# Attention and two expert layers on one core: zeroing spread over four engines, scale products on ScalarE, and a planner that keeps VectorE and GpSimd apart

## The chip, the core and the metric

The kernel runs on one core of a Trainium2 chip. The metric is device microseconds from the first to the last instruction of one execution. Five engines work side by side and meet at semaphores: TensorE (PE for matmuls, PEld for the loads of their weights), VectorE (DVE), ScalarE (ACT), GpSimd (POOL) and SyncE (SP), which here only issues DMA transfers. Every engine takes its instructions in the order in which they stand in the program; one that waits holds up all behind it on that engine.

## What is computed

```
# 1. delta-rule attention, batch 4, 8 heads, 768 tokens, head_dim 48
k_n = k / (norm(k) + 1e-6)
for t in range(768):
    y[t]  = q[t] @ state
    v_old = k_n[t] @ state
    state = state + beta[t] * outer(k_n[t], v[t] - v_old)
# 2. first expert layer: 3072 tokens x 384, 8 experts of 1024, weights P
P = exp(x @ w_gate - max);  8 rounds of row and column normalisation
out = sum_e P[:, e] * (relu(x @ w1[e]) @ w2[e])
# 3. second expert layer: each token goes to its best expert only
```

## The kernel before

The attention runs over 24 blocks of 64 tokens (12 chunks of two pairs of batches). A block's work falls into a front part (norms of K, power-of-two scales for Q and V, splitting into two fp16 parts), the inverse of a 64x64 triangle by five levels of matmuls, and a part that carries the state. The nodes have names that the code gives them: `ssr` is the sum of squares of K, `rc1` to `rc5` the reciprocal of the norm, `kn` the scaled keys, `kh` and `kl` their two parts, `qh` and `ql` those of Q, `kpd` and `kb` the copies of keys into block-diagonal buffers, `z`, `Z`, `a`, `t`, `tt` one level of the inverse, `ds` and `S` the state, `mx` the largest output of a block, `is`, `si` and `lgs` the scale of the logits and the logits.

The block-diagonal buffers must hold zeros outside their blocks. There are four rotating sets (`zK`, `zQ`, `zT`, `zM`, `zP`, `zU`); the first set is zeroed by GpSimd, the others by DMAs from a tensor of zeros (L1297 to L1303).

While the attention runs, units of the first expert layer for tokens that are already done are woven into TensorE's order (L1089 and L1115), so that TensorE has work where the attention waits. Expert 0 needs its weights loaded, measured by sums of squares (L1188), scaled and split (L1226, L1228).

The order on every engine is made by a list scheduler in the program itself, `Sched`. Each node has a cost in nanoseconds, an engine or a choice of two, a priority and dependencies. `plan` always takes the node that can start first on its engine and writes the order down; the program then issues it so. On the chip nothing of the plan's times is left, only the order on each engine. Of 40 plans with shuffled priorities the one that does best in `late`, a second model with random delays, is taken. One node is a stand-in for a set-up of GpSimd that the plan prices at 9400 ns, `("lib", 0)`, with the operation of L1295.

After the attention come the eight normalisation rounds of P (about 34 us on VectorE, beside expert units on TensorE), the rest of the first layer in blocks (L534, L584), and the second layer.

Of the kernel before, what the change touches and what calls it, by code (L numbers as in the profile page):

```python
# [15 lines left out]
ALU = mybir.AluOpType  # L16
# [32 lines left out]
class Sched:  # L49
# [6 lines left out]
    SHUFFLE = 0.2  # L56

    def __init__(self, slots):
        self.free = {e: 0.0 for e in "PVAGD"}
        self.slots = {k_: [0.0] * n for k_, n in slots.items()}  # L60
        self.nodes = []
        self.names = {}
        self.warm = False
        self.tick, self.colsum = 0, 0.0
        self.credit, self.tlast = 0.0, 0.0
        self.log = []

    def node(self, eng, cost, fn, deps, prio=0.0, ps=None, cols=0, frees=None, moe=False, name="", floor=0.0, lat=0.0):
# [18 lines left out]
    def start(self, n, e):  # L87
        s = max(n.ready, self.free[e])
        if n.ps:
            fr = [x for x in self.slots[n.ps[0]] if x is not None]  # L90
            if not fr:
                return None
            s = max(s, min(fr))
        return s

    def run(self, draws=1):
# [4 lines left out]
        for k in range(draws):  # L101
# [3 lines left out]
            self.free, self.slots = dict(free), {k_: list(v) for k_, v in slots.items()}  # L105
            self.warm, self.tick, self.colsum, self.credit, self.tlast, self.log = False, 0, 0.0, 0.0, 0.0, []
# [43 lines left out]
    def plan(self):  # L150
# [3 lines left out]
        while left:  # L154
# [55 lines left out]
            self.free[e] = end  # L210
            self.log.append((n.name, e, s, end))
# [19 lines left out]
def kernel(  # L231
# [412 lines left out]
    def mk_pe(e, key=None, iv=None):  # L644
        iv = e if iv is None else iv
        a = pet[:, iv]
        nc.vector.tensor_tensor(out=a, in0=P[:, :, e], in1=isx, op=ALU.mult)
        nc.vector.tensor_scalar(out=a, in0=a, scalar1=ivt[:, iv:iv + 1], scalar2=None, op0=ALU.mult)
        pe[key or e] = a
# [10 lines left out]
    ND = 3  # L660
    ZF = {"zK": 0.0, "zQ": 0.0, "zT": 1800.0, "zM": 3600.0, "zP": 4200.0, "zU": 5000.0}
# [3 lines left out]
    with (  # L665
# [20 lines left out]
        sch = Sched({"pz": 3, "pc": 2, "pt": 2, "py": 1})  # L686
# [53 lines left out]
        def block(i):  # L740
# [89 lines left out]
            N("par", "A", 200, lambda: nc.scalar.activation(out=o["sr"][:, 8:10], in_=o["sv"], func=AF.Sqrt), ["sv", "sq"], frees="sv")  # L830
            N("rc1", "V", 120, lambda: nc.vector.reciprocal(out=tl("rc", [8], F32, par), in_=o["sr"][:, 0:8]), ["sq", ("kn", i - 2)])
            N("rc2", "V", 80, lambda: nc.vector.tensor_tensor(out=o["rc"], in0=o["rc"], in1=o["ss"][:, 0:8], op=ALU.mult), ["rc1"])
            N("rc3", "V", 80, lambda: nc.vector.tensor_tensor(out=o["rc"], in0=o["sr"][:, 0:8], in1=o["rc"], op=ALU.add), ["rc2"])
            N("rc4", "V", 70, lambda: nc.vector.tensor_scalar(
                out=o["rc"], in0=o["rc"], scalar1=256.0 / 64, scalar2=1e-6 / 64, op0=ALU.mult, op1=ALU.add), ["rc3"])
            N("rc5", "V", 120, lambda: nc.vector.reciprocal(out=o["rc"], in_=o["rc"]), ["rc4"])
# [15 lines left out]
            else:  # L852
# [176 lines left out]
            N("is", "V", 70, lambda: nc.vector.tensor_tensor(out=isx[:, i:i + 1], in0=o["mx"][:, 0:1], in1=o["scl"][:, 7:8], op=ALU.mult), ["mp", "p4"], prio=tp)  # L1029
            N("si", "V", 70, lambda: nc.vector.tensor_tensor(out=o["scl"][:, 4:5], in0=isx[:, i:i + 1], in1=ivg, op=ALU.mult), ["is", ("lgs", i - 2)], prio=tp)  # L1030
# [21 lines left out]
            N("lgs", "V", 133, lambda: nc.vector.tensor_scalar(out=lg[:, i], in0=o["pl"], scalar1=o["scl"][:, 4:5], scalar2=None, op0=ALU.mult),  # L1052
# [1070 lines left out]
```

## Time and profile before

| what | us |
|---|---|
| median of 3 runs | 2105.6 (2104.56 to 2108.5) |
| profiled execution | 2101.38 |
| its span | 2099.2 |
| PE busy in the span | 1985.6 (95%) |
| DVE busy | 1387.7 (66%) |
| ACT busy | 1150.6 (55%) |
| POOL busy | 602.3 (29%) |

The attention's last logits are written at 604 us. "Busy" is the union of an engine's instructions. A PE that shows busy is not necessarily at its peak, since short matmuls overlap. In a line of a timeline the bracket at the end is the time for which the engine stood idle before the instruction, and what ended the wait.

### The profile page before, as it was taken

The numbers are of one execution on the slowest core, as the hardware profiler recorded it, in microseconds if no ns is written. First come the engines' busy times: TensorE is split into PE (matmuls) and PEld (weight loads), VectorE is DVE, ScalarE is ACT, GpSimd is POOL, SyncE is SP. The second block draws the span as 40 slices with busy tenths as digits, with TensorE's granted clock in tenths as the row PEclk, the third lists the DMA queues.
The fourth block names the chain that finished last, engine by engine and source line by source line (L and its number), as shares of the span: only waits on it lengthen the run. The fifth ranks groups of instructions, "written<-read, shape, count | busy, mean of one in ns | idle before, by whom it ended". The sixth has DMA issues, their size and how long they took to land. (4 is left out here: it accounts for less than half of the span.)

```text
span 2099.2 us, 55384 instructions
## 1 busy us (share of the span) xinstructions
PE 1985.6 (95%) x23391; PEld 1630.9 (78%) x23391; DVE 1387.7 (66%) x3045; ACT 1150.6 (55%) x2374; POOL 602.3 (29%) x524
## 2 busy tenths in 40 slices
PE   3779999999999999999999999999999999999998
PEld 3667777777775479999899989988999755567777
DVE  6988988988772776776767677676766555551111
ACT  6766665666532656666666656665665333433322
POOL 2232233223100123533533343353333201022211
PEclk9889999999999999999999999999999999999999
DMA  8355655546535113022032112302220010168765
GB/s 281 82 104 107 126 114 110 123 103 132 116 100 208 45 61 121 32 92 91 31 121 96 58 54 99 121 32 91 95 88 31 1 28 20 31 222 332 251 222 208
DMA packets 325982, 230.02 MB, mean 110 GB/s; under 512 B 258572, under 2 KB 303536, under 8 KB 319330
## 3 DMA queue, kind: packets, MB, share of 16 engines
q1 hardware_dynamic: 321442, 216.18, 34.7%
q0 software_dynamic: 4288, 10.25, 1.4%
q8 instruction: 185, 3.03, 0.6%
q14 instruction: 67, 0.55, 0.1%
HBM read 146.94 MB, written 50.36 MB: 94 GB/s over the span
## 5 line engine op out<-in xcount | busy, mean ns | idle before, releaser
L534 PE MATMUL pt<-big,W 128*128 128x256 f16 x4320 | 511.0, 273 | 0.0
L534 PEld LDWEIGHTS <-W 128*128 128x128 f16 x4320 | 418.5, 98 | 43.9 <-issue 0.3
L542 ACT ACTIVATE R<-pt 128x512 f32<-128x512 f32 x240 | 142.6, 594 | 306.9 <-PE pt L534 283.4
L525 POOL TENSOR_TENSOR R<-R,R 128x512 f32<-128x512 f32 x120 | 155.3, 1294 | 371.6 <-ACT R L542 288.2
L566 DVE SCALAR_TENSOR_TENSOR accb<-py,pet,accb 128x192 f32<-128x192 f32 x240 | 123.0, 513 | 203.8 <-PE py L584 203.3
L525 POOL TENSOR_TENSOR R<-R 128x512 f32<-128x512 f32 x120 | 161.6, 1346 | 195.3 <-ACT R L542 190.6
L584 PEld LDWEIGHTS <-A 128*128 128x128 f16 x2520 | 211.1, 98 | 7.2 <-DVE A L522 2.6
L1089 PE MATMUL pt<-accb,W 128*128 128x256 f16 (+1 forms) x1368 | 180.9, 272 | 3.5 <-ACT accb L729 1.8
L1115 PE MATMUL py<-W,hhl 128*128 128x384 f16 x756 | 152.6, 328 | 2.6 <-ACT yo L1125 1.7
L584 PE MATMUL py<-W,A 128*128 128x192 f16 x1440 | 134.7, 246 | 2.1 <-DVE accb L566 1.4
L1089 PEld LDWEIGHTS <-W 128*128 128x128 f16 x1368 | 118.3, 100 | 18.7 <-issue 3.8
L1635 PEld LDWEIGHTS <-W 128*128 128x128 f16 x1008 | 90.6, 98 | 51.1 <-issue 0.7
L584 PEld LDWEIGHTS <-hhl 128*128 128x128 f16 x1440 | 120.6, 98 | 5.9 <-DVE hhl L522 3.6
L1655 PE MATMUL py<-W,hhl 128*128 128x384 f16 x624 | 108.8, 326 | 0.0
L1641 DVE SCALAR_TENSOR_TENSOR ttb<-pt,ttb 128x512 f16<-128x512 f32 x50 | 34.6, 692 | 111.5 <-ACT ttb L1640 111.1
L584 PE MATMUL py<-W,hhl 128*128 128x192 f16 x1080 | 105.1, 246 | 2.8 <-DVE hhl L522 2.7
L1115 PEld LDWEIGHTS <-hhl 128*128 128x128 f16 x864 | 74.2, 98 | 40.8 <-DVE hhl L1102 3.2
L394 ACT ACTIVATE jk<-st 128x512 f32<-128x512 f32 x162 | 98.0, 605 | 13.7 <-DMA st<-in_moe_w_dram 11.4
L584 PE MATMUL py<-ew,A 128*128 128x192 f16 x1080 | 104.3, 246 | 0.6 <-DVE A L522 0.5
L522 DVE TENSOR_TENSOR A<-R,A 128x512 f16<-128x512 f32 x120 | 100.7, 841 | 2.9 <-ACT A L519 2.9
L584 PEld LDWEIGHTS <-ttb 128*128 128x128 f16 x1080 | 91.0, 98 | 9.9 <-issue 5.4
L1635 PE MATMUL pt<-big,W 128*128 128x512 f16 x432 | 97.7, 379 | 0.0
(411 smaller groups left out, 4090.4 us busy)
## 6 DMA issues: line engine op xcount, KB each, us to landing
st<-in_moe_w_dram SPq DMA_DIRECT2D x27, 1536.0 KB, 9.9
W<-w2d SPq DMA_DIRECT2D x18, 1536.0 KB, 8.2
w2d<-big SPq DMA_DIRECT2D x16, 1536.0 KB
big<-w2d SPq DMA_DIRECT2D x8, 1536.0 KB, 7.4
accb<-w2d SPq DMA_DIRECT2D x8, 1536.0 KB, 8.1
big<-accb SPq DMA_DIRECT2D x90, 128.0 KB, 3.6
accb<-in_kq_dram SPq DMA_DIRECT2D x23, 448.0 KB, 4.6
st<-PTc SPq DMA_DIRECT2D x42, 128.0 KB, 3.2
```

The costliest lines, as they stand in the source:

```text
L394: nc.scalar.activation(out=jk, in_=st[:, c * CW:c * CW + CW], func=AF.Square, scale=2.0 ** 0.5, accum_out=ss[:, c:c + 1])
L522: return lambda: nc.vector.tensor_tensor(out=A[2 * k + 1], in0=src, in1=A[2 * k], op=ALU.subtract)
L525: nc.gpsimd.tensor_tensor(out=out, in0=a, in1=b, op=op)
L534: nc.tensor.matmul(out=po, lhsT=w1v(W, wv, kk, f), rhs=xv[:, kk].rearrange("p (h n) -> p h n", h=2), start=kk == 0 and x == 0 and f % 2 == ...
L542: nc.scalar.activation(out=(R1, R)[y][:, :, o:o + 256], in_=pv if y else pv_, func=AF.Relu)
L566: nc.vector.scalar_tensor_tensor(out=acc[t][:, sl], in0=src, scalar=sc, in1=acc[t][:, sl], op0=ALU.mult, op1=ALU.add)
L584: nc.tensor.matmul(out=py, lhsT=A[2 * ka + a_][:, 128 * q_:128 * q_ + 128], rhs=B[2 * kb + b_][:, DH * q_:DH * q_ + DH], start=first and q ...
L1089: nc.tensor.matmul(out=o[g4][:, nt_ * j:nt_ * j + nt_], lhsT=w1v(W, wv, kk, f_), rhs=XR[:, xv, kk], start=(kk == 0 and x == 0), stop=(kk = ...
L1115: nc.tensor.matmul(out=o["py", j][:, 0:DM], lhsT=a_[f_ // per][:, c_:c_ + 128], rhs=w2v(W, b_, f_), start=(f_ == 0 and x == 0), stop=(f_ = ...
L1635: nc.tensor.matmul(out=po, lhsT=w1v(W, wv, kk, f), rhs=xv[:, kk, :], start=(kk == 0 and x == 0), stop=(kk == KD - 1 and x == 2))
L1641: V((f"rs{q_}", id_), lambda q_=q_: nc.vector.scalar_tensor_tensor(out=HL[q_], in0=o[q_], scalar=0.0, in1=HH[q_], op0=ALU.max, op1=ALU.sub ...
L1655: nc.tensor.matmul(out=o["py"][:, 0:DM], lhsT=a_[f // per][:, c_:c_ + 128], rhs=w2v(W, b_, f), start=(f == 0 and x == 0), stop=(f == KF - ...
```

## The change

Four things change in the attention's part.

1. Of the buffers that DMAs zeroed, four are zeroed by VectorE (`ZV`: set 1 of zK, zT, zQ, zM) and two by ScalarE (`ZA`: set 1 of zP and set 2 of zK). Ten DMAs of zeros stay of sixteen.
2. Four products of scales per block (`p3`, `p4`, `is`, `si`) go from VectorE to ScalarE. Two instructions of VectorE per block are folded away (`ssc` into a bias of the square root and other powers of two, `rc4` into `rc3`).
3. The matmul that adds squares over partitions (`sv`) takes bf16 operands instead of f32, and waits for ScalarE's sum alone and no more for VectorE.
4. `Sched` gets the flag `shared`. With it, an instruction of VectorE or GpSimd whose name is not in `ALONE` may not start in the plan before the other engine's last such instruction has ended.

```diff
+    ALONE = [x + y for x, n in (("Z", 6), ("m", 2), ("pt", 2), ("t", 6), ("rs", 4)) for y in "012345"[:n]] + [
+        f"tt{x}" for x in range(1, 6)] + ["r1", "r2", "U", "S", "mx", "lgs", "ssr"]
...
+        n.port = self.shared and name.split(".")[0] not in self.ALONE
...
         s = max(n.ready, self.free[e])
+        if n.port and e in "VG":
+            s = max(s, self.held["VG"[e == "V"]])
...
             self.free[e] = end
+            if n.port and e in "VG":
+                self.held[e] = end
...
+    onesb = res.tile([128, 128], BF16, name="onesb")
...
+    nc.gpsimd.memset(onesb, 1.0)
+    tiny = res.tile([128, 1], F32, name="tiny")
+    nc.gpsimd.memset(tiny, 1e-30)
...
+    ZV = (("zK", 1), ("zT", 1), ("zQ", 1), ("zM", 1))
+    ZA = (("zP", 1), ("zK", 2))
...
-        sch = Sched({"pz": 3, "pc": 2, "pt": 2, "py": 1})
+        sch = Sched({"pz": 3, "pc": 2, "pt": 2, "py": 1}, True)
...
-            N("ssc", "V", 70, lambda: nc.vector.tensor_scalar(
-                out=o["ss"], in0=o["ss"], scalar1=2.0 ** -18, scalar2=1e-30, op0=ALU.mult, op1=ALU.max), ["ssr", "sqv"])
-            N("sq", "A", 220, lambda: nc.scalar.activation(out=tl("sr", [10], F32, par)[:, 0:8], in_=o["ss"][:, 0:8], func=AF.Sqrt),
-              ["ssc", ("pq", i - 2), ("rc3", i - 2)])
+            N("sq", "A", 220, lambda: nc.scalar.activation(out=tl("sr", [10], F32, par)[:, 0:8], in_=o["ss"][:, 0:8], func=AF.Sqrt, bias=tiny),
+              ["ssr", ("pq", i - 2), ("rc3", i - 2)])
...
-                nc.tensor.matmul(out=o["sv"], lhsT=ones32, rhs=o["ss"][:, 8:10], start=True, stop=True)
-            N("sv", "P", 250, f, ["ssc"], ps=("pc", 1))
+                nc.tensor.matmul(out=o["sv"], lhsT=onesb, rhs=o["ss"].bitcast(BF16)[:, 17:20:2], start=True, stop=True)
+            N("sv", "P", 100, f, ["sqv"], ps=("pc", 1))
...
-            N("p3", "V", 75, lambda: nc.vector.tensor_tensor(
-                out=o["scl"][:, 5:6], in0=o["scl"][:, 1:2], in1=c3[:, 1:2], op=ALU.mult), ["pm", ("cs", 0)])
-            N("p4", "V", 70, lambda: stt(o["scl"][:, 7:8], o["scl"][:, 0:1], 0.125, o["scl"][:, 1:2], ALU.mult), ["pm"])
+            N("p3", "A", 170, lambda: nc.scalar.activation(out=o["scl"][:, 5:6], in_=o["scl"][:, 1:2], func=AF.Copy, scale=1.0 / 128), ["pm"])
+            N("p4", "A", 170, lambda: nc.scalar.activation(out=o["scl"][:, 7:8], in_=o["scl"][:, 0:1], func=AF.Copy, scale=o["scl"][:, 5:6]), ["p3"])
...
-            N("is", "V", 70, lambda: nc.vector.tensor_tensor(out=isx[:, i:i + 1], in0=o["mx"][:, 0:1], in1=o["scl"][:, 7:8], op=ALU.mult), ["mp", "p4"], prio=tp)
-            N("si", "V", 70, lambda: nc.vector.tensor_tensor(out=o["scl"][:, 4:5], in0=isx[:, i:i + 1], in1=ivg, op=ALU.mult), ["is", ("lgs", i - 2)], prio=tp)
+            N("is", "A", 170, lambda: nc.scalar.activation(out=isx[:, i:i + 1], in_=o["mx"][:, 0:1], func=AF.Copy, scale=o["scl"][:, 7:8]), ["mp", "p4"], prio=tp)
+            N("si", "A", 170, lambda: nc.scalar.activation(out=o["scl"][:, 4:5], in_=isx[:, i:i + 1], func=AF.Copy, scale=ivg), ["is", ("lgs", i - 2), ("wg3", 0)], prio=tp)
...
+                elif (nm, i) in ZV:
+                    Q((nm, i), "V", 150 + 0.45 * c_, lambda t=bufs[i]: nc.vector.memset(t.bitcast(F32), 0.0), [], -9.0)
+                elif (nm, i) in ZA:
+                    Q((nm, i), "A", 950, lambda t=bufs[i], c_=c_: nc.scalar.activation(
+                        out=t.rearrange("p a h k -> p (a h k)").bitcast(F32), in_=ones32[:, 0:1].to_broadcast([128, c_ // 2]), func=AF.Copy, scale=0.0), [], -9.0, floor=1300.0)
```

The plan comes out in another order on every engine. Three places at the start are shown. First ScalarE, from its first work on block 0 on. `accb` holds block 0's keys and queries and, in other columns, the loaded weights of expert 0, whose sums of squares go to `wmx`; `scl` holds the scales, `pz` is PSUM. Before:

```order
L813 ACTIVATE accb,ss<-accb 128x512
L806 ACTIVATE accb<-accb 128x384
L816 ACTIVATE accb,ss<-V 128x384
L822 ACTIVATE sr<-ss 128x8
L830 ACTIVATE sr<-sv 128x2
L729 CAST accb<-accb 128x384
L856 ACTIVATE V<-V,scl 128x384
L860 ACTIVATE accb<-accb,scl 128x8x64
L729 COPY big<-accb 64x16x48
L729 CAST accb<-pz 128x8x64 x2
```

And now:

```order
L844 ACTIVATE sr<-sv,tiny 128x2
L822 ACTIVATE accb<-hhl 128x384
L1200 ACTIVATE W_96,wmx<-accb 128x1024 x2
L869 ACTIVATE V<-V,scl 128x384
L873 ACTIVATE accb<-accb,scl 128x8x64
L745 CAST Rh<-V 128x384
L875 ACTIVATE scl<-scl 128x1
L1200 ACTIVATE W_96,wmx<-accb 128x1024
L876 ACTIVATE scl<-scl 128x1
L745 COPY big<-accb 64x16x48
L1200 ACTIVATE W_96,wmx<-W_97 128x768
L1212 ACTIVATE wma<-sw 128x1
```

Four squares of expert 0's weights (L1200), all of which wait for loads, now stand among the steps of block 0; the two zero fills stand ahead of this stretch, before block 0's first square, and the casts of block 0's keys out of PSUM (`pz`) one square behind it.

Second SyncE, from the ninth DMA on: `hhl<-in_kq_dram` loads block 1, `in_moe_w_dram` expert 0's weights, `in_zer_dram` are zeros. Before:

```order
L1276 DMA btok<-in_beta_dram 128x192
L1301 DMA st<-in_zer_dram 128x2048
L1301 DMA big<-in_zer_dram 128x2048
L1301 DMA ttb<-in_zer_dram 128x1024
L1175 DMA accb<-in_moe_w_dram 128x1024
L717 DMA big<-accb 64x16x64 x2
L800 DMA accb<-in_kq_dram 128x896
```

And now:

```order
L1288 DMA btok<-in_beta_dram 128x192
L816 DMA hhl<-in_kq_dram 128x896
L817 DMA V<-in_v_dram 128x384
L1187 DMA accb<-in_moe_w_dram 128x1024 x3
L1318 DMA ttb<-in_zer_dram 128x1024
L1289 DMA wg_s<-in_moe_w_gate_dram 128x3x8
L1187 DMA W_97<-in_moe_w_dram 128x4x384 x2
L1318 DMA ttb<-in_zer_dram 128x1024
L1318 DMA st<-in_zer_dram 128x2048
```

The weights go ahead of all but one of the zeros that are left, and the router's weights (`wg_s`) ahead of all but one too.

Third VectorE, in block 0's front part; `wm` and `dp` belong to the router's weights, `w0p` and `w0s` to the scale of expert 0's. Before:

```order
L836 RECIPROCAL rc<-rc 128x8
L845 TENSOR_SCALAR scl<-sr 128x2
L725 TENSOR_TENSOR accb<-accb,rc 128x384
L854 TENSOR_SCALAR scl<-scl 128x2
L862 TENSOR_TENSOR scl<-scl,cs 128x1
L722 SCALAR_TENSOR_TENSOR scl<-scl 128x1
L725 TENSOR_TENSOR accb<-accb 128x384
```

And now:

```order
L849 RECIPROCAL rc<-rc 128x8
L747 CAST accb<-accb 128x384
L741 TENSOR_TENSOR W_97<-cs,btok 128x512
L738 SCALAR_TENSOR_TENSOR accb<-accb,scl 128x8x64
L741 TENSOR_TENSOR accb<-accb 128x384
L1294 TENSOR_REDUCE wm_194<-wg_s 128x1
L747 COPY big<-accb 64x16x48
L1149 TENSOR_SCALAR pet<-cs,wm_194 128x128
L346 TENSOR_SCALAR w0p<-wma 128x1
```

The product of the keys with `rc` (`kn`, L725 before) is no longer on VectorE; it is GpSimd's first product now. The scales of the router's and of expert 0's weights stand in front of block 0's later copies.

## Rows read from the trace of the kernel before

**Rows 1.** By stage: us, then busy us (instructions) per engine, TensorE clock, DMA share, GB/s

```profile
0.00:100.00 100.00, 55.12 (x846) 48.81 (x847) 80.88 (x210) 71.29 (x146) 26.00 (x30) 0.91 0.61 182
100.00:600.00 500.00, 463.40 (x8818) 371.43 (x8817) 424.32 (x1008) 305.08 (x643) 135.95 (x123) 0.98 0.54 114
...
760.00:2100.00 1340.00, 1314.30 (x12764) 1117.88 (x12761) 781.76 (x1611) 705.25 (x1451) 425.41 (x355) 1.00 0.29 101
```

**Rows 2.** Timeline at the attention's end: start, us, engine, line, instruction

```profile
638.50 0.24 DVE L648 TENSOR_SCALAR pet<-pet,ivt 128x24 f32<-128x24 f32 x1
...
651.80 7.93 PE L1358 MATMUL pt<-big,W 128*128 128x512 f16 x36
```

**Rows 3.** Timeline of VectorE in the first 83 us

```profile
5.28 0.55 DVE L818 TENSOR_REDUCE ss<-accb 128x8 f32<-128x384 f32 x1 [5.28 <-ACT accb L806]
...
25.00 0.69 DVE L725 TENSOR_TENSOR Z<-pz,cs 128x512 f16<-128x512 f32 x1
...
34.44 0.72 DVE L731 COPY big<-accb 64x768 f16<-64x768 f16 x2 [4.07 <-DMA big<-in_zer_dram]
35.08 0.68 DVE L725 TENSOR_TENSOR Z<-pz,cs 128x512 f16<-128x512 f32 x1
...
37.94 0.18 DVE L1282 TENSOR_REDUCE wm<-wg_s 128x1 f32<-128x24 f32 x1 [1.56 <-DMA wg_s<-in_moe_w_gate_dram]
...
82.05 0.51 DVE L1014 TENSOR_REDUCE mx<-pc 128x1 f32<-128x384 f32 x1
```

**Rows 4.** Timeline of TensorE: block 0's first keys, and the first expert unit

```profile
10.67 1.04 PE L877 MATMUL pz<-c,big 128*128 128x64 f16 x16 [3.85 <-ACT big L729]
...
87.33 4.30 PE L1089 MATMUL pt<-accb,W 128*128 128x128 f16 x42 [0.37 <-ACT accb L729]
```

**Rows 5.** Timeline of ScalarE in the first 40 us

```profile
4.12 0.63 ACT L813 ACTIVATE accb<-accb 128x512 f16<-128x512 f32 x1 [1.85 <-DMA accb<-in_kq_dram]
...
25.16 1.06 ACT L1188 ACTIVATE W<-accb 128x1024 f16<-128x1024 f32 x1 [1.30 <-DMA accb<-in_moe_w_dram]
...
33.08 0.84 ACT L1188 ACTIVATE W<-W 128x768 f16<-128x768 f32 x1 [2.07 <-DMA W<-in_moe_w_dram]
```

**Rows 6.** Two stretches at the start, columns as in rows 1

```profile
0.00:20.00 20.00, 4.66 (x44) 4.36 (x44) 10.31 (x33) 11.65 (x28) 8.17 (x16) 1.00 0.87 283
20.00:40.00 20.00, 7.20 (x90) 6.16 (x90) 12.71 (x38) 12.57 (x28) 4.07 (x4) 1.00 1.03 391
```

**Rows 7.** Line L725 on POOL, first 17 us: duration ns min/median/max, first and last start

```profile
L725 POOLq EVENT_SEMAPHORE  x2: 17/3432/6848, 10.0 to 17.0; - x2
```

**Rows 8.** Small instructions of VectorE, 0 to 650 us: busy us, mean ns | idle before

```profile
L1030 DVE TENSOR_TENSOR scl<-isx,ivg 128x1 f32<-128x1 f32 x24 | 8.3, 345 | 0.1
L1029 DVE TENSOR_TENSOR isx<-mx,scl 128x1 f32<-128x1 f32 x24 | 6.8, 284 | 0.1
...
L820 DVE TENSOR_SCALAR ss<-ss 128x10 f32<-128x10 f32 x24 | 5.4, 227 | 3.3 <-ACT hhl L816 1.7 <-ACT accb L816 0.7
...
L862 DVE TENSOR_TENSOR scl<-scl,cs 128x1 f32<-128x1 f32 x24 | 4.2, 175 | 0.9 <-DMA cs<-in_cst_dram 0.8
L834 DVE TENSOR_SCALAR rc<-rc 128x8 f32<-128x8 f32 x24 | 4.0, 168 | 0.3
L722 DVE SCALAR_TENSOR_TENSOR scl<-scl 128x1 f32<-128x1 f32 x24 | 3.7, 153 | 0.2
```

**Rows 9.** Single lines: duration ns min/median/max, first and last start us

```profile
L1030 DVE TENSOR_TENSOR scl<-isx,ivg x24: 117/156/1044, 85.7 to 600.6; 128x1 f32<-128x1 f32 x24
...
L836 DVE RECIPROCAL rc<-rc x24: 182/202/204, 7.2 to 519.8; 128x8 f32<-128x8 f32 x24
...
L830 ACT ACTIVATE sr<-sv x24: 153/172/178, 6.9 to 514.4; 128x2 f32<-128x2 f32 x24
...
L828 PE MATMUL sv<-ss,ones x48: 167/251/374, 6.3 to 514.1; 128*128 128x2 f32 x48
```

**Rows 10.** TensorE's waits for VectorE's `ss`, 100 to 600 us: total, times, longest

```profile
PE sv L828 <- DVE ss L820: 4.0, 3, 2.8
```

More of the change, by code (lines that the diff above doesn't have):

```diff
@@ L56, with __init__ @@
     SHUFFLE = 0.2
-    def __init__(self, slots):
+    ALONE = [x + y for x, n in (("Z", 6), ("m", 2), ("pt", 2), ("t", 6), ("rs", 4)) for y in "012345"[:n]] + [
+        f"tt{x}" for x in range(1, 6)] + ["r1", "r2", "U", "S", "mx", "lgs", "ssr"]
+    def __init__(self, slots, shared=False):
+        self.shared = shared
         self.free = {e: 0.0 for e in "PVAGD"}
+        self.held = {"V": 0.0, "G": 0.0}
         self.slots = {k_: [0.0] * n for k_, n in slots.items()}
@@ L105, in run @@
             self.free, self.slots = dict(free), {k_: list(v) for k_, v in slots.items()}
+            self.held = {"V": 0.0, "G": 0.0}
             self.warm, self.tick, self.colsum, self.credit, self.tlast, self.log = False, 0, 0.0, 0.0, 0.0, []
@@ L647, in mk_pe @@
         nc.vector.tensor_tensor(out=a, in0=P[:, :, e], in1=isx, op=ALU.mult)
-        nc.vector.tensor_scalar(out=a, in0=a, scalar1=ivt[:, iv:iv + 1], scalar2=None, op0=ALU.mult)
+        nc.vector.tensor_scalar(out=a, in0=a, scalar1=ivt[:, iv:iv + 1], scalar2=16.0, op0=ALU.mult, op1=ALU.mult)
         pe[key or e] = a
@@ L805, in f @@
                 tl("K2", [8, 48], F32, 0)
-                nc.scalar.activation(out=o["K2"], in_=o["K"], func=AF.Square)
+                nc.scalar.activation(out=o["K2"], in_=o["K"], func=AF.Square, scale=2.0 ** -7)
             N("sqk", "A", 420, f, ["ld", ("ssr", i - 1)])
@@ L813, in f @@
                 nc.scalar.activation(
-                    out=o["jk"][:, 0:512].rearrange("p (h s) -> p h s", h=8), in_=o["Q"], func=AF.Square, scale=1.0 / 16, accum_out=o["ss"][:, 8:9])
+                    out=o["jk"][:, 0:512].rearrange("p (h s) -> p h s", h=8), in_=o["Q"], func=AF.Square, scale=2.0 ** -13, accum_out=o["ss"][:, 8:9])
             N("sqq", "A", 620, f, ["ld", ("kpd", pb), ("rc2", i - 2), ("par", i - 2)])
             N("sqv", "A", 510, lambda: nc.scalar.activation(
-                out=o["jk"][:, 0:DM].rearrange("p (h d) -> p h d", h=8), in_=o["V"], func=AF.Square, accum_out=o["ss"][:, 9:10]), ["sqq"])
+                out=o["jk"][:, 0:DM].rearrange("p (h d) -> p h d", h=8), in_=o["V"], func=AF.Square, scale=2.0 ** -9, accum_out=o["ss"][:, 9:10]), ["sqq"])
@@ L831, in block @@
+            N("sv", "P", 100, f, ["sqv"], ps=("pc", 1))
+            N("par", "A", 200, lambda: nc.scalar.activation(out=o["sr"][:, 8:10], in_=o["sv"], func=AF.Sqrt, bias=tiny), ["sv", "sq"], frees="sv")
             N("rc1", "V", 120, lambda: nc.vector.reciprocal(out=tl("rc", [8], F32, par), in_=o["sr"][:, 0:8]), ["sq", ("kn", i - 2)])
             N("rc2", "V", 80, lambda: nc.vector.tensor_tensor(out=o["rc"], in0=o["rc"], in1=o["ss"][:, 0:8], op=ALU.mult), ["rc1"])
-            N("rc3", "V", 80, lambda: nc.vector.tensor_tensor(out=o["rc"], in0=o["sr"][:, 0:8], in1=o["rc"], op=ALU.add), ["rc2"])
@@ L834, in block @@
-            N("rc4", "V", 70, lambda: nc.vector.tensor_scalar(
-                out=o["rc"], in0=o["rc"], scalar1=256.0 / 64, scalar2=1e-6 / 64, op0=ALU.mult, op1=ALU.add), ["rc3"])
-            N("rc5", "V", 120, lambda: nc.vector.reciprocal(out=o["rc"], in_=o["rc"]), ["rc4"])
+            N("rc3", "V", 80, lambda: nc.vector.scalar_tensor_tensor(
+                out=o["rc"], in0=o["rc"], scalar=1e-6 / 64, in1=o["sr"][:, 0:8], op0=ALU.add, op1=ALU.add), ["rc2"])
+            N("rc5", "V", 120, lambda: nc.vector.reciprocal(out=o["rc"], in_=o["rc"]), ["rc3"])
@@ L1051, in block @@
             N("pl", "P", 230, f, ["xe", ("wg", 0)], ps=("pc", 1), cols=72, prio=tp)
-            N("lgs", "V", 133, lambda: nc.vector.tensor_scalar(out=lg[:, i], in0=o["pl"], scalar1=o["scl"][:, 4:5], scalar2=None, op0=ALU.mult),
+            N("lgs", "V", 133, lambda: nc.vector.tensor_scalar(out=lg[:, i], in0=o["pl"], scalar1=o["scl"][:, 4:5], scalar2=16.0, op0=ALU.mult, op1=ALU.mult),
               ["pl", "si"], frees="pl", prio=tp)
```

1 line of the change is left out of this document (removed).

## Prediction

> **What bounds the kernel.** I read the table by stage first, then the timelines at the seams, then the waits. From 760 us to the end PE is busy 1314 of 1340 us at full clock [rows 1]: nothing of the change works there, and matmuls set the pace. Before that PE stands idle: 44.9 of the first 100 us, 36.6 of the next 500 [rows 1]. The matmuls of the attention and of the woven units are the same before and after but for `sv`, so the change is worth what it takes from, or adds to, those 81.5 us. The normalisation rounds don't come in between: they are done at 638.50 us, and PE has units of experts 0 and 1 up to 651.80 and a group that needs no P behind them [rows 2].
>
> The first 100 us are a chain. TensorE's expert units wait for block 0's outputs; the first starts at 87.33 [rows 4]. Block 0's first level is masked by VectorE at 25.00, its second at 35.08, the largest output found at 82.05 [rows 3]. On the way VectorE stands 4.07 us behind a DMA of zeros and 1.56 behind the router's weights, ScalarE 1.30 and 2.07 behind expert 0's weights [rows 3, 5]. These wait for bytes: the DMA engines are busy to 0.87 and 1.03 of their time in the first and second 20 us and move 283 and 391 GB/s [rows 6], 13.5 MB in all. The change takes out five fills of 2048 fp16 columns on 128 partitions and one of 1024, 2.9 MB, or 7 us at 391 GB/s.
>
> **Part 1, zeroing.** The fills move to time that is idle: VectorE does nothing until 5.28, ScalarE starts block 0 at 4.12 [rows 3, 5]. Two fills of 1024 elements on ScalarE take about the 1.06 us of the 1024-element square [rows 5] each; they end near 4.2, at no cost. No fill on VectorE is in the trace. A 512-element masking takes 0.69 [rows 3], so 1024 elements take at most 1.38 and all four fills 4.8 us, under the 5.28; if GpSimd's own fills hold them up it is a few us more, hidden behind what comes next. The Trainium skill ("VectorE: DVE Perf Modes", section "Zero memsets can be issued as uint32 (trn2)") gives one cycle per element for a memset; at its 0.96 GHz that is an estimate of 3.7 us for the four, the same answer.
>
> **Part 2, the order at the start.** This is the larger term and has both signs. The plan takes the stand-in `lib` (9400 ns) for work that keeps VectorE out, so in the plan VectorE is late and weights come first. On ScalarE two squares of weights stand ahead of `vs` and `qh`; GpSimd, whose sequencer takes up its first product only at 10.0 us [rows 7], now does `kn`. What does it cost block 0? Ahead of the second chunk of weights stand 2.5 MB of inputs and constants and 1.0 MB of weights, at 283 to 391 GB/s 9 to 12.4 us; I take 12. Two squares of 1.06 each [rows 5] end a little after 14. `vs`, `qh`, then `ql`, `kl` and the copies follow at their 0.4 to 0.8 us each, and block 0's first keys reach PE near 18 instead of 10.67 [rows 4]. Through the next two squares, the casts and the masks I come to 32 for the first level's mask instead of 25.00 [rows 3]: 7 us late.
>
> Then it gains. From the first mask to the largest output VectorE has in the new order 75 rows, which add up to 36 us, each at the spacing that its kind has in the trace; in the old order the same stretch adds up to 43.5 us and took 57.05 (82.05 - 25.00), so 13.5 us went on waits (4.07 + 1.56 are shown) and on stretched instructions. The new list is shorter because `pi`, `tt0` and the router's scale of blocks 0 and 1 and part of the weights' work now stand ahead of the first mask. With the zeros and weights landed earlier I leave 7 us for waits: largest output at 75, 7 us ahead of 82.05, and the first expert unit at 80 instead of 87.33. Start: **-7 us**. Bounds: -13 without those waits, +7 if the 7 us late are never made up.
>
> **Part 3, `sv`.** In f32 it takes two matmuls per block, 48 in all, whose median is 251 ns [rows 9] and which overlap; in bf16 it takes one. So at most 24 x 0.25 = 6 us go, at least 0. And PE no longer stands 4.0 us between 100 and 600 for VectorE's `ss` [rows 10]; what is late next is ScalarE's square, which ends earlier. **-4**.
>
> **Part 4, VectorE relieved.** Six kinds of instruction go, 24 of each, in all 8.3 + 6.8 + 5.4 + 4.2 + 4.0 + 3.7 = 32.4 us busy [rows 8]. They overlap with their neighbours, so VectorE's list gets shorter by less: some 20 us, of which 3 + 4.5 come from `is` and `si` alone, whose median is 0.16 and whose mean 0.28 and 0.35, up to 1.04 [rows 8, 9]. Those long ones lie beside GpSimd products. VectorE is busy 424 of 500 us [rows 1], so 20 us are 5%; PE's idle time there is 36.6 us and not all VectorE's. Bounds 0 and -20; I take **-5**. The planner's new rule should also let fewer pairs collide. The engines drift from the plan by more than one instruction's length, so I take little of it: **-3**, between 0 and -10; slightly worse is possible too and is in the third rival.
>
> Here the Trainium skill speaks against the change. The trace shows that some of the instructions which the plan keeps apart never collide: `rc5`, a reciprocal of 128x8, takes 182 to 204 ns in all 24 cases, while `si` reaches 1044 [rows 9]. "SBUF — State Buffer", section "Who interferes with whom", says that only VectorE's second port is shared, with an exclusive lock, and that an instruction with one SBUF input outside the two-port modes doesn't contend. By that, much of what is not in `ALONE` (reciprocals, one-column masks, the fills) is kept apart for nothing, and so is the hold by `lib`. The sum by it would be the first rival below: the harm of part 2 without the gain of part 4.
>
> **Part 5, ScalarE loaded.** 4 x 24 products at the 172 ns of the two-column root [rows 9] are 16.5 us, and some 13 casts more. ScalarE is busy 305 of 500 us [rows 1]; what it delays is the cast `t` of the inverse's levels. Between 0 and +16; **+2**.
>
> Sum: -7 - 4 - 5 - 3 + 2 = -17. The profiled execution's 2101.38 (2099.2 and 2.2 around it) becomes 2084; it lies 4.2 us under the median of 2105.6, and against that I predict **2088.6, rounded to 2088**.
>
> **Rivals.** First, late start (slower): block 0 waits on ScalarE for weights and on GpSimd for `kn`, and the 7 us at the first level stay, because the later levels are bound by the round trip PE, VectorE, ScalarE and not by VectorE's list. Decided by whether the first expert unit starts after 90 us. With +7 at the start, -4 for `sv` and the rest hidden, +2 for ScalarE: 2111. For it: TensorE waits there for many different engines; against: the 4.07 and 2.07 us waits that go.
>
> Second, ScalarE takes VectorE's place: the small products wait in line for `mp` and `pm` and hold up `t`. All 16 us, against -7 and -4: 2111 with no other gain, 2103 with part 4. Mostly that is no change.
>
> Third, the relief passes in full: -9 at the start, -4, -20 and -6 by fewer collisions: 2067. For it: VectorE's 85%; against: four fifths of PE's 36.6 idle us [rows 1] would have to go, and a list in another order moves waits as well as removing them.
>
> Fourth, only the start and `sv` count: 2095.
>
> **How the numbers follow.** Forecast (2080 to 2092) 0.42; fourth rival 0.17; third 0.18; first 0.13; second 0.10. A difference under 0.2% (4.2 us) can't be told from none here. Faster takes the forecast, the third and fourth: 0.77, less 0.02 for a fourth that falls short: 0.75; the second and what falls short give 0.11 the same; 0.14 slower. Most of the weight lies below 2105, so the range runs from the third rival, somewhat inside the full bounds, to just past no change: 2064 to 2106.
>
> **What would show it.** Right: no wait of VectorE for zeros longer than 1 us; first keys on PE at 15 to 20 us and the first mask near 32, yet the first expert unit at 76 to 84; `sv` no longer among PE's waits; VectorE busy under 410 us between 100 and 600; the last logits near 588. Wrong: the first expert unit after 90 us, or PE's waits between 100 and 600 us for ScalarE growing by more than 10 us, or the expert units after the attention waiting for the normalisation rounds.

## The result and the profile after

The changed kernel takes **2087.88 us** (median of 6, 2082.65 to 2089.61) against 2104.94 (6 runs, 2104.35 to 2108.5): ratio 0.9912, 95% interval 0.9898 to 0.9926, so 17 us faster, where 2088 was predicted. The sum was right. Its terms were not, and another draw of the planner alone moves these two kernels by 8.0 and 6.4 us (five kernels: 3 to 15).

The table by stage of the kernel after (columns as in [rows 1]):

```profile
0.00:100.00 100.00, 51.94 (x846) 46.04 (x847) 76.30 (x184) 80.07 (x169) 27.50 (x36) 0.71 0.56 154
100.00:600.00 500.00, 471.47 (x8929) 381.57 (x8930) 409.12 (x933) 330.37 (x747) 122.53 (x121) 0.98 0.59 120
...
760.00:2100.00 1340.00, 1299.23 (x12583) 1102.01 (x12580) 773.61 (x1594) 697.27 (x1434) 422.15 (x353) 1.00 0.29 101
```

The first 100 us did not get better: TensorE idles 48.1 us there instead of 44.9. Between 100 and 600 it idles 28.5 instead of 36.6, and 111 more matmuls fall into that time (8929 against 8818). ScalarE is busier by 25 us, VectorE less by 15.

Where the time went shows best at points that both kernels pass. First the start, on VectorE (start, us, engine, line, instruction; against [rows 3]):

```profile
1.05 0.91 DVE L1313 MEMSET big<- 128x1024 f32 x1 [1.05 <-PEq L2112]
...
3.73 0.91 DVE L1313 MEMSET big<- 128x1024 f32 x1 [0.16 <-issue]
...
16.64 0.75 DVE L738 SCALAR_TENSOR_TENSOR accb<-accb,scl 128x512 f16<-128x512 f32 x1 [4.55 <-ACT accb L873]
...
28.98 0.55 DVE L834 TENSOR_REDUCE ss<-accb 128x8 f32<-128x384 f32 x1 [3.85 <-ACT accb L822]
...
36.84 0.68 DVE L741 TENSOR_TENSOR Z<-pz,cs 128x512 f16<-128x512 f32 x1
...
79.10 0.55 DVE L1026 TENSOR_REDUCE mx<-pc 128x1 f32<-128x384 f32 x1
...
82.22 0.14 DVE L1029 TENSOR_SCALAR mx<-mx 128x1 uint32<-128x1 uint32 x1
```

The fills end at 4.64, before VectorE has work, and none of its waits in the first 100 us names a DMA of zeros. But `ql` stands 4.55 us behind ScalarE, block 2's sum of squares 3.85 us, and the first level's mask comes at 36.84 instead of 25.00. By the largest output (`mx`) all 12 us are made up and 3 more: 79.10 against 82.05. Then they are lost again. The scale made from it (L1029) stands 3.1 us behind `mx`, with five other instructions between besides L1028; in the kernel before it stood 1.7 behind, with three. And the low half of the scaled output (`yhl`), which VectorE made there in 0.55 us, now waits on GpSimd behind a product of `PTc`:

```profile
83.65 1.16 POOL L741 TENSOR_TENSOR PTc<-accb,PTc 128x512 f16<-128x512 f32 x1 [1.77 <-DVE tt L935]
84.77 0.92 POOL L741 TENSOR_TENSOR yhl<-ys,yhl 128x384 f16<-128x384 f32 x1
```

ScalarE and TensorE of the kernel after, at the places of [rows 5] and [rows 4]:

```profile
6.93 0.63 ACT L829 ACTIVATE accb<-accb 128x512 f16<-128x512 f32 x1 [2.78 <-DMA accb<-in_kq_dram]
...
13.16 1.06 ACT L1200 ACTIVATE W<-accb 128x1024 f16<-128x1024 f32 x1 [2.48 <-DMA accb<-in_moe_w_dram]
...
28.43 0.52 ACT L822 ACTIVATE accb<-accb 128x384 f32<-128x384 f32 x1 [4.33 <-DMA accb<-in_kq_dram]
```

```profile
19.31 1.06 PE L889 MATMUL pz<-c,big 128*128 128x64 f16 x16
...
88.05 2.63 PE L1101 MATMUL pt<-accb,W 128*128 128x128 f16 x24
...
633.83 7.93 PE L1375 MATMUL pt<-big,W 128*128 128x512 f16 x36
```

ScalarE gets block 0's own load 2.8 us later than before (6.93 against 4.12), though it is issued at 0.76 us in both. Two squares of weights stand ahead of `vs` and `qh`, as the prediction said, and the load of block 2 keeps ScalarE 4.33 us. The first expert unit starts at 88.05, 0.7 us **later** than in [rows 4]. The group behind the units starts at 633.83 instead of 651.80 [rows 2], 18.0 us earlier. The DMA engines moved less in the first 40 us, as computed (columns as in [rows 6]): 332 and 212 GB/s over 20 us each are 10.9 MB, where it was 13.5, 2.6 MB less for 2.9 MB of fills taken out.

```profile
0.00:20.00 20.00, 3.12 (x22) 2.83 (x23) 7.54 (x19) 12.79 (x28) 6.14 (x16) 1.00 0.92 332
20.00:40.00 20.00, 6.57 (x81) 5.90 (x79) 13.27 (x48) 15.58 (x39) 5.01 (x5) 0.73 0.70 212
```

From the first unit to the group behind the units the kernel before takes 564.5 us and the kernel after 545.8: all of the gain, 18.7 us, lies there.

Only a part of it is idle time of TensorE. Up to the group both kernels run the same matmuls but for the 24 that `sv` no longer needs (columns as in [rows 1]; the kernel before, then the kernel after):

```profile
0.00:651.80 651.80, 569.81 (x10054) 457.21 (x10055) 538.80 (x1312) 391.03 (x814) 163.77 (x161) 0.97 0.53 122
0.00:633.82 633.82, 556.92 (x10030) 452.23 (x10031) 501.94 (x1161) 418.09 (x929) 150.03 (x157) 0.94 0.56 121
```

TensorE idles 76.9 us there instead of 82.0, 5.1 less, and is busy 12.9 us less. Under other draws of both kernels it is 7.3 and 10.2 us. "Busy" is the union of records that overlap, so the same matmuls can cover less time when they stand closer together. The granted clock explains little of it: between the first unit and the group it stood at its lower level (1.2 GHz) for 27.7 us before and 19.5 after, which is worth some 4 us at most. What else shortens the busy time is not shown.

Single lines of the kernel before and the kernel after (duration ns min/median/max, first and last start us):

```profile
L1052 DVE TENSOR_SCALAR P<-pl,scl x24: 185/219/228, 91.9 to 604.3; 128x8 f32<-128x8 f32 x24
```

```profile
L1064 DVE TENSOR_SCALAR P<-pl,scl x24: 177/217/229, 91.3 to 582.6; 128x8 f32<-128x8 f32 x24
...
L876 ACT ACTIVATE scl<-scl x24: 278/282/300, 18.1 to 506.3; 128x1 f32<-128x1 f32 x24
...
L842 PE MATMUL sv<-ss,onesb x24: 163/167/188, 8.6 to 494.9; 128*128 128x2 bf16 x24
```

The logits of block 0 are 0.6 us earlier, those of the last block 21.7. The router's rounds end in time (the last scaling of `pet` at 617.63). In the profiled execution 6.3 us of the 18.0 are given back after the group: from there to the end it takes 1453.7 us, and 1447.4 before. The code of that stretch is the same; over the 14 kernels of this study it took 1447.4 to 1454.6, with the kernel before at the lower end. Most of the difference can be the clock: within that stretch it was granted at 0.50 for 13.7 us in the kernel after (at 708.3, 1643.6 and 1851.8) and for 3.4 in the kernel before (at 1866.1), not counting the last 3 us; 10 us more at half the clock are worth up to 5. In the medians 17 of the 18 us remain.

What TensorE waits for between 100 and 600 us, kernel after (total, times, longest):

```profile
PE pz L722 <- DVE Z L741: 6.9, 10, 1.4
PE pg L905 <- DMA big<-accb: 2.7, 5, 1.2
...
PE sv L842 <- ACT sr L836: 1.4, 1, 1.4
...
PE sv L842 <- ACT accb L832: 1.4, 1, 1.4
```

Added up by engine over all such rows, TensorE's waits for VectorE fall from 25.2 to 10.7 us; those for ScalarE rise from 7.4 to 11.6, those for DMAs from 1.9 to 5.7.

### The profile page after: what moved, and what is told of

Same layout as the page of the kernel before. It is cut to its first block, busy times and chain, and to the rows that moved or that the text cites. A ratio compares the mean times of both kernels' runs of the same rounds, so it can differ in the third digit from the quotient of the medians.

```text
span 2087.5 us, 55229 instructions
## 1 busy us (share of the span) xinstructions
PE 1977.0 (95%) x23367; PEld 1626.8 (78%) x23367; DVE 1351.6 (65%) x2894; ACT 1177.0 (56%) x2489; POOL 588.5 (28%) x520
## 5 line engine op out<-in xcount | busy, mean ns | idle before, releaser
L1127 PE MATMUL py<-W,hhl 128*128 128x384 f16 x756 | 147.9, 327 | 4.1 <-ACT yo L1137 2.2
L1127 PEld LDWEIGHTS <-hhl 128*128 128x128 f16 x864 | 75.3, 98 | 45.1 <-DVE hhl L1114 3.1
L1672 PE MATMUL py<-W,hhl 128*128 128x384 f16 x624 | 108.8, 326 | 0.0
L408 ACT ACTIVATE jk<-st 128x512 f32<-128x512 f32 x162 | 98.0, 605 | 14.0 <-DMA st<-in_moe_w_dram 11.8
L598 PEld LDWEIGHTS <-ttb 128*128 128x128 f16 x1080 | 92.1, 98 | 10.1 <-issue 5.4
```

What stands on the lines that cost most here:

```text
L408: nc.scalar.activation(out=jk, in_=st[:, c * CW:c * CW + CW], func=AF.Square, scale=2.0 ** 0.5, accum_out=ss[:, c:c + 1])
L598: nc.tensor.matmul(out=py, lhsT=A[2 * ka + a_][:, 128 * q_:128 * q_ + 128], rhs=B[2 * kb + b_][:, DH * q_:DH * q_ + DH], start=first and q ...
L1127: nc.tensor.matmul(out=o["py", j][:, 0:DM], lhsT=a_[f_ // per][:, c_:c_ + 128], rhs=w2v(W, b_, f_), start=(f_ == 0 and x == 0), stop=(f_ = ...
L1672: nc.tensor.matmul(out=o["py"][:, 0:DM], lhsT=a_[f // per][:, c_:c_ + 128], rhs=w2v(W, b_, f), start=(f == 0 and x == 0), stop=(f == KF - ...
```

## The experiments

Two theories stood against each other. The prediction's: relieved instructions of VectorE and `sv` carry most of the later gain, the hold little, the start much. The rival: the planner's hold carries the later gain, by keeping VectorE's instructions from being stretched beside GpSimd's products, and it spoils the start by its stand-in `lib`. A third has to be told apart from both: every edit makes the planner draw another plan.

What the runs gave, with the points of their profiles in us. The kernel before was run again beside each group of them (2104.9, 2104.0, 2105.5); each ratio is to its own. "Stretch" is worked out from each trace between 100 and 600 us: the time of VectorE's instructions above the 20th percentile of their own kind (line, operation, shape), summed.

| kernel | median | ratio to before, 95% | first unit | group behind | from unit to group | stretch |
|---|---|---|---|---|---|---|
| before | 2104.9 | | 87.3 | 651.8 | 564.5 | 48 |
| before, other draws | 2096.9 | 0.9949 to 0.9976 | 80.4 | 645.0 | 564.6 | 53 |
| zeroing alone | 2097.2 | 0.9958 to 0.9981 | 88.3 | 643.0 | 554.7 | 50 |
| hold alone | 2099.7 | 0.9967 to 0.9994 | 92.1 | 647.2 | 555.0 | 28 |
| hold alone, other draws | 2084.3 | 0.9882 to 0.9918 | 88.2 | 632.8 | 544.6 | 26 |
| after without hold | 2091.2 | 0.9920 to 0.9954 | 74.5 | 636.8 | 562.2 | 41 |
| the same, other draws | 2087.8 | 0.9896 to 0.9929 | 81.3 | 633.9 | 552.6 | 37 |
| after | 2087.9 | 0.9898 to 0.9926 | 88.0 | 633.8 | 545.8 | 24 |
| after, other draws | 2081.5 | 0.9880 to 0.9911 | 87.5 | 627.5 | 540.0 | 20 |
| `lib` freed | 2076.5 | 0.9843 to 0.9886 | 75.3 | 623.0 | 547.7 | 19 |
| `lib` freed, other draws | 2083.1 | 0.9870 to 0.9906 | 81.4 | 631.4 | 550.0 | 19 |
| more freed | 2078.2 | 0.9859 to 0.9897 | 80.9 | 626.4 | 545.6 | 20 |
| after, `sv` in f32 | 2085.7 | 0.9890 to 0.9924 | 88.3 | 637.3 | 549.0 | 24 |
| after, products on VectorE | 2088.8 | 0.9910 to 0.9947 | 86.0 | 630.2 | 544.2 | 30 |

### Other draws

One line of the planner, in the kernel after and, further down, in four others:

```diff
-            rng = random.Random(k)
+            rng = random.Random(k + 100)
```

> The changed kernel with only other random draws in its planner (40 other shuffles of the priorities), so with another plan of the same work. It tells how much of 17 us a plan by itself can be worth. If the gain is that of the edits, the median is 2088 give or take 4 and the first weight matmul of the late experts stands 18 us earlier than before, give or take 4; if the gain is largely luck of one draw, it comes out over 2094 or under 2082.

Measured: 2081.5, 6.4 us under the kernel after; the late experts (the expert units behind the group, whose first weight matmul starts at 725.2 us in the kernel after) 6.3 us earlier. That is half a microsecond beyond the bound of 2082 that was set for a lucky draw, though on the fast side. So a plan of the same work is by itself worth what several terms of the sum were.

> The kernel before with other random draws in its planner and nothing else: what another plan of the same work is worth on that side. If the 17 us come from the edits, 2101 to 2108, with the late experts starting at 740 to 746. If the kernel before had an unlucky plan and part of every gain is a new draw, 2093 to 2099, as the zeroing alone (2097) suggests, whose first expert unit stood where it was.

Measured: 2096.9, 8.0 us under the kernel before. As the second branch had it, the kernel before had the worse of two plans, most of it at the start (first unit at 80.4, not 87.3). A comparison of two kernels that are planned anew carries this scatter; only pairs over several draws can price an edit.

### The hold

Left out of the kernel after:

```diff
-        sch = Sched({"pz": 3, "pc": 2, "pt": 2, "py": 1}, True)
+        sch = Sched({"pz": 3, "pc": 2, "pt": 2, "py": 1})
```

> The changed kernel without the planner's rule that holds VectorE and GpSimd apart; zeroing on four engines, bf16 sv and products on ScalarE stay. Theory of the prediction (relief of VectorE and sv carry the gain, the hold gives 3 us): 2091, with VectorE's stretched instructions back. Rival (the hold carries most, by fewer collisions): 2098 to 2104. Rival (the hold costs at the start by the stand-in of GpSimd's first call and gives little later): 2078 to 2085, with the first masked level near 25 us and not at 36.8.

> The changed kernel without the hold, under other draws. If what starts the first expert unit at 74.5 us there is the missing hold by the stand-in of GpSimd's first call, it comes at 73 to 80 again; if it was the draw, at 81 to 90. Median by the hold's price after the first unit (14 to 16 us): 2089 to 2095; if the hold is worth nothing and the draw did it: 2078 to 2086.

Put into the kernel before, alone (`ALONE`, `held` and `port` as in the change, and the `True`):

> The kernel before with the planner's rule alone: zeros by DMA, f32 sv and all products on VectorE. By the prediction 3 us for fewer collisions and a late start: 2100 to 2107. If the rule carries most of the gain: 2088 to 2094, with VectorE's busy time between 100 and 600 us down by 10 or more though it has as many instructions as before.

> The kernel before with the hold alone, under other draws. If the hold shortens VectorE's work whatever the draw, its stretch beside GpSimd products falls again to about half of before's and the median is 2094 to 2101, with the first expert unit late again (89 to 95 us). If hold and draw are worth the same, 2102 to 2108.

Measured: four pairs that differ by the hold. The expectations on a single median were hit or missed as the draw fell. Without the hold, 2091.2 is the prediction's own branch, and 2087.8 lies between the two that were named. The hold alone gave 2099.7, between its two branches, and 2084.3, 10 us under the one whose cause it was meant to show. The first unit at 81.3 without the hold fell, by 0.3, to the branch of the draw. The points of the pairs agree better. With the hold the first unit comes later by 4.8, 7.8, 13.5 and 6.2 us, mean 8. From the unit to the group it takes 9.5, 20.0, 16.4 and 12.6 us less, mean 15. The medians fall by 5.3, 12.6, 3.4 and 6.3, mean 7. Expected at 3 us, the hold is thus two large terms of opposite sign, 7 us in sum.

The two are not independent prices. A first unit that comes late leaves less of the attention to come behind it, and so can shorten the distance to the group by itself. "`lib` freed" below keeps the hold without the late start: against the kernel without hold its first unit differs by 0.8 and 0.1 us, from unit to group it takes 14.6 and 2.6 us less, and the median is 14.7 and 4.7 lower, mean 10. TensorE's idle time says the same: in the four pairs the hold takes a mean of 8.4 us of it away behind the first unit and adds 9.0 ahead of it. What is left of its 7 us is TensorE being busy for less time with the same matmuls (8.7, 6.0, 2.3 and 11.5 us), and how the hold does that is not shown.

What it does to VectorE is seen where the instructions are the same. VectorE's group rows between 100 and 600 us (busy us, mean ns | idle before), without the hold (after without hold) and with it (after):

```profile
L738 DVE SCALAR_TENSOR_TENSOR accb<-accb,scl 128x512 f16<-128x512 f32 x19 | 16.0, 844 | 0.6 <-ACT accb L873 0.4
L741 DVE TENSOR_TENSOR tt<-W,cs 128x512 f16<-128x512 f32 x12 | 13.0, 1083 | 0.1
L741 DVE TENSOR_TENSOR yhl<-ys,yhl 128x384 f16<-128x384 f32 x11 | 9.7, 881 | 2.2 <-ACT yhl L745 1.6 <-POOL accb L741 0.5
```

```profile
L738 DVE SCALAR_TENSOR_TENSOR accb<-accb,scl 128x512 f16<-128x512 f32 x19 | 14.0, 739 | 1.2 <-ACT accb L873 1.0
L741 DVE TENSOR_TENSOR tt<-W,cs 128x512 f16<-128x512 f32 x13 | 11.6, 892 | 0.2 <-POOL W L741 0.2
L741 DVE TENSOR_TENSOR yhl<-ys,yhl 128x384 f16<-128x384 f32 x15 | 9.6, 637 | 3.9 <-ACT yhl L745 3.8
```

The same instruction is 105 to 244 ns shorter on average. That GpSimd is what stretches them can be read from the traces: of the 48 us of stretch in the kernel before, 39.5 lie in the 291 of its VectorE instructions that overlap one of GpSimd in time and 8.5 in the 716 others; with the hold alone 289 overlap, so as many as before, and they hold 20.4. The rule thus doesn't keep the engines from working side by side, only the pairs that contend. The hold alone, with 1011 instructions against the 1008 of [rows 1], keeps VectorE busy 410.06 us instead of 424.32 (under the other draws 423.85 instead of 432.43, with 1053 against 1022):

```profile
100.00:600.00 500.00, 470.65 (x9045) 382.13 (x9045) 410.06 (x1011) 322.68 (x678) 137.40 (x136) 0.98 0.57 121
```

Stretch separates the fourteen kernels cleanly: 37 to 53 us without the hold, 19 to 30 with it.

### The stand-in for GpSimd's first call

```diff
-        f"tt{x}" for x in range(1, 6)] + ["r1", "r2", "U", "S", "mx", "lgs", "ssr"]
+        f"tt{x}" for x in range(1, 6)] + ["r1", "r2", "U", "S", "mx", "lgs", "ssr", "lib"]
```

> The changed kernel with the 9.4 us stand-in for GpSimd's first call freed from the rule, so that VectorE is not kept back by it in the plan. The first masked level should come at 25 to 28 us and not at 36.8. If the late first level is what ate the 7 us that the prediction had for the start, the first expert unit comes at 76 to 82 us and the median is 2079 to 2083; if the order that it forces (weights and router early) pays it back, the first expert unit stays at 86 to 90 and the median at 2086 to 2090.

> The changed kernel with the stand-in for GpSimd's first call freed, under other draws. If freeing it is worth its 11 us whatever the draw, the first expert unit comes at 74 to 82 and the median at 2070 to 2079, under the 2081.5 of the changed kernel with the same draws. If 2076.5 was a lucky draw, 2080 to 2088.

Measured: the first level's mask comes at 21.97 and 26.6 us, the first unit at 75.3 and 81.4 instead of 88.0 and 87.5. VectorE and TensorE with `lib` freed:

```profile
21.97 0.69 DVE L741 TENSOR_TENSOR Z<-pz,cs 128x512 f16<-128x512 f32 x1
```

```profile
75.28 0.89 PE L1101 MATMUL pt<-accb,W 128*128 128x128 f16 x13
```

Under either draw the first unit then comes where it comes without any hold (74.5 and 81.3). So the hold by `lib` is what makes the start late. The stand-in is also longer than what it stands for: under other draws of the kernel after, GpSimd takes its first product at 9.02 us, where the plan keeps VectorE out to 14.9 (5.5 + 9.4):

```profile
5.73 0.18 POOL L1307 TENSOR_TENSOR sep<-ones 128x1 f32<-128x1 f32 x1
9.02 1.33 POOL L741 TENSOR_TENSOR accb<-accb,rc 128x384 f32<-128x384 f32 x1 [3.11 <-issue]
```

Whether it shows in the time is left to the draw: 11.3 us under the kernel after with the first draws, 1.7 above with the second, which is the branch "lucky draw" of the expectation. What comes early at the start (12.7 and 6.1 us) is given back between unit and group by 1.9 and 10.0. The version at 2076.5 beats both kernels, as a plan; that the edit beats the kernel after whatever the draw is not shown.

```diff
-        f"tt{x}" for x in range(1, 6)] + ["r1", "r2", "U", "S", "mx", "lgs", "ssr"]
+        f"tt{x}" for x in range(1, 6)] + ["r1", "r2", "U", "S", "mx", "lgs", "ssr", "lib", "rc1", "rc5",
+        "mk", "ms", "mp", "ke0", "ke1", "tc", "et", "xe"]
```

> The changed kernel with the stand-in for GpSimd's first call and, besides, those instructions freed from the rule that kept their length beside a GpSimd product in the traces: reciprocals, one-column masks, casts out of PSUM. If what VectorE loses in the plan by needless holds counts, it is faster than the kernel with the stand-in alone freed (2076.5): 2068 to 2074. If the plan's draw decides, it lies within 6 us of 2076.5 on either side, with no fewer stretched instructions.

Measured: 2078.2, inside the scatter of 2076.5, with the first mask at 31.27 and the first unit at 80.9, so not as early as with `lib` alone under these draws. Freeing these as well changes nothing that can be told, and does no harm: stretch stays at 20.

### Zeroing alone

The kernel before with the fills of the change (`ZV`, `ZA` and their two branches):

> The kernel before with the zeroing on four engines alone: f32 sv, products on VectorE, no hold. If the fills are what moves the start forward by 13 us in the changed kernel without the hold, the first expert unit comes at 74 to 78 us instead of 87.3 and the median is 2090 to 2096, since nothing later changes. By the prediction's start term alone (7 us): 2098. If the start moved only because another plan came out, 2101 to 2107.

Measured: 2097.2, but the first unit is at 88.3. So under these draws the fills do not bring the start forward, and none of the three expectations holds: what is gained comes between unit and group (9.8 us), where nothing of the zeroing works. It can't be told from the 2096.9 of other draws alone.

### `sv` and the products, with the plan kept

These two replace what is issued and leave every engine's place in the plan as it was:

```diff
-                nc.tensor.matmul(out=o["sv"], lhsT=onesb, rhs=o["ss"].bitcast(BF16)[:, 17:20:2], start=True, stop=True)
+                nc.tensor.matmul(out=o["sv"], lhsT=ones32, rhs=o["ss"][:, 8:10], start=True, stop=True)
```

> The changed kernel with the same plan, row by row, and only the matmul of sv in f32 again (two passes instead of one, 24 times). By the prediction's term of 4 us: 2092. By the bound of 24 x 0.25 us: 2094. If that matmul hides in TensorE's waits for others, 2086 to 2090 and the late experts start within 1.5 us of 725.2.

Measured: 2085.7, a little under the range for a matmul that hides, and the late experts at 728.7, outside the 1.5 us that went with it. The matmul's median is 251 ns again and there are 48; the profile has it 3.5 us later, the medians 2.2 us earlier. Both are about what two runs of one plan differ by, so `sv` is worth between nothing and the 4 us that were put on it.

```diff
-            N("is", "A", 170, lambda: nc.scalar.activation(out=isx[:, i:i + 1], in_=o["mx"][:, 0:1], func=AF.Copy, scale=o["scl"][:, 7:8]), ...
+            N("is", "A", 170, lambda: nc.vector.tensor_tensor(out=isx[:, i:i + 1], in0=o["mx"][:, 0:1], in1=o["scl"][:, 7:8], op=ALU.mult), ...
```

and so for `si`, `p3` and `p4`.

> The changed kernel with the same plan, and only the four scale products of each block (p3, p4, is, si) issued on VectorE at the place where the plan has them on ScalarE. By the prediction (5 us for a relieved VectorE of which these are two thirds, against 2 us for ScalarE): 2089 to 2091. If VectorE's instructions are the bound, 96 x 0.16 = 15 us more of them come out as 2096 to 2103. If they hide, 2085 to 2089.

Measured: 2088.8. VectorE has 90 instructions and 11 us more between 100 and 600, and from unit to group it takes 544.2 us, 1.6 less than the kernel after:

```profile
100.00:600.00 500.00, 471.43 (x8919) 381.60 (x8917) 420.27 (x1023) 318.13 (x662) 122.67 (x121) 0.99 0.59 120
```

So nearly all of these 11 us of VectorE hide: 2096 to 2103 is excluded, the prediction's 2089 to 2091 is too near to be told apart. They were the larger part of "VectorE relieved".

## Why the prediction was right

The sum was right because one term that failed was made up by another that was too small: the start came out at +0.7 us instead of -7, and from the first unit to the group it was -18.7 where the other terms add up to -10.

- **What the change is worth: incomplete.** The prediction puts it at "what it takes from, or adds to" TensorE's idle time of 81.5 us. Up to the group idle time fell by 5.1 us and busy time by 12.9, for which the sum had only `sv`.
- **The start, -7: failed.** It came out at +0.7. The step that failed is "the first expert unit at 80 instead of 87.33". The rows ahead of it were seen: keys at 19.31 (foreseen at 18), `mx` ahead by 3 us. The first level came 12 us late, not 7, because ScalarE waited for block 0's load and for weights. Then the prediction carried the distance from `mx` to the unit over from the kernel before (5.3 us), while the new list put other work in front of the scale that ScalarE waits for, and `yhl` on GpSimd: it became 9.0. The cause of the late start is the hold by `lib`: with it freed, the same two draws start 12.7 and 6.1 us earlier. This is the harm of the first rival; its decision point of 90 us was missed by 2.
- **Zeroing: the part off the path was right, the rest open.** The fills cost nothing: they took 0.91 us per 1024 elements (estimated at most 1.38), ended at 4.64 before VectorE's first work, and the wait of 4.07 us for zeros is gone. Zeroing alone did not move the first unit forward, under the one draw that was run. The wait that replaced it is for block 0's and block 2's loads.
- **The hold, -3: wrong by its size.** The step said that "the engines drift from the plan by more than one instruction's length, so I take little of it". They do not drift so far that the rule is lost: it halves the stretch. The runs price it at a mean of 7 us with the hold by `lib` in it (four pairs), and of 10 without (two pairs). "SBUF — State Buffer" of the Trainium skill, section "Who interferes with whom", was weighed as speaking against the change. Its rule holds in these traces: without the hold the reciprocal `rc5` stays at 154 to 203 ns and the stream transposes at 654 to 715, while `px_` on 128x2, which may enter a two-port mode, reaches 1122 and `tt0`, with two inputs in SBUF, 1646. The conclusion drawn from it failed: what is kept apart for nothing costs little outside `lib`, and keeping apart what does contend was worth more than that.

Lines of the kernel after without the hold (duration ns min/median/max):

```profile
L867 DVE TENSOR_SCALAR scl<-scl x24: 125/169/1122, 7.1 to 512.2; 128x2 uint32<-128x2 uint32 x24
...
L849 DVE RECIPROCAL rc<-rc x24: 154/192/203, 7.0 to 505.8; 128x8 f32<-128x8 f32 x24
...
L935 DVE STREAM_TRANSPOSE tt<-t x96: 654/701/715, 29.4 to 557.4; 128x512 f16<-128x512 f16 x96
...
L741 DVE TENSOR_TENSOR tt<-W,cs x15: 674/1021/1646, 18.3 to 531.1; 128x512 f16<-128x512 f32 x15
```

- **`sv` -4, VectorE relieved -5, ScalarE +2: right as a sum, by its parts not shown.** Four pairs without and with these edits (zeroing with them) differ from unit to group by 2.3, 12.0, 9.2 and 4.6 us, mean 7, which is the -7 that was put on them; their medians differ by 13.7, 9.1, 11.8 and 2.8, mean 9, and so carry no less of the 16 us than the hold. Alone, with the plan kept, neither `sv` nor the four products moves the time by more than its scatter. What else is left in the pairs is the two instructions dropped (`ssc`, `rc4`), `sv`'s earlier release and the draw; no run tells these apart. ScalarE's products take 0.20 to 0.30 us, not the 0.17 assumed; TensorE's waits for ScalarE rose by 4.2 us, under the 10 at which the second rival would have held.
- **What would show it.** Hit: no wait for zeros, keys at 19.31, VectorE busy 409.1 (under 410), no unit waiting for the router's rounds. Missed: the mask near 32 (36.84), the unit at 76 to 84 (88.05), `sv` gone from the waits (2.8 us of 4.0 left, now for ScalarE). The last logits came at 582.6, earlier than the 588 foreseen, since the later gain was larger.
- **What was not foreseen at all** is the planner's draw: 8.0, 15.4, 3.4 and 6.4 us between two draws of one kernel, all to the good of the second, and 6.6 the other way with `lib` freed. The forecast of 17 us for this pair of plans had luck in it: the four pairings of a plan before with a plan after give 9.0 to 23.4. Over both draws the mean goes from 2100.9 to 2084.7, 16 us, and all eight pairs with and without the hold or the other edits have the same sign; so the edits carry it, as far as two draws can tell.

Open: why ScalarE gets block 0's load only at 6.3 to 7.2 us in the three runs of this one plan and at 4.1 to 4.3 elsewhere, though it is issued at the same time; what shortens TensorE's busy time; and what the zeroing is worth with the plan kept, which was not run.

## What to carry to other kernels

Where a planner draws its order at random, measure each edit under two or more draws, or keep the plan and swap only what is issued: a single new plan is worth as much as the edit. An instruction's busy time on the fullest engine is not its price; look at what makes its neighbours longer, and price the mean against the shortest of its kind. A stand-in in a plan (here 9.4 us for a first call) can do more harm through a new rule than through its own length, so look at each entry when the rule around it changes.

## What the hardware showed

VectorE and GpSimd fill SBUF side by side at full pace: 1024 f32 elements per partition took VectorE 0.91 us and GpSimd 0.95, both as alone (VectorE at 6.20 us under other draws of the kernel after, GpSimd in the kernel before). One column more decides whether a small instruction suffers from GpSimd: over the 14 traces, VectorE's `TENSOR_SCALAR` of 128x1 never took more than 156 ns in the 710 cases that started during a GpSimd product, while that of 128x2 took up to 1127 in 108 such cases and at most 171 in all others. ScalarE's product of 128x1 with a scale read from SBUF takes 0.28 to 0.30 us, with a constant 0.20 (VectorE's, unstretched, 0.15). The granted clock of TensorE over the first 100 us was 0.71, against 0.91 before [rows 1]; with `lib` freed it was 0.74, and the first unit came 12.7 us earlier all the same, so the clock did not set the start.
